# Block-sparse attention and gated MLP on one core: pair 2 before pair 3, block rows by GpSimd as 32-bit words, mask products in one bank, first transposes regrouped

## The chip, the cores and the metric

One core of a Trainium2 chip runs the whole program in one launch. The metric is the device time in microseconds (us). Five engines work side by side, each through its own instructions in order: TensorE (PE, with its weight loads as PEld), VectorE (DVE), ScalarE (ACT), GpSimd (POOL), and SyncE (SP), whose queue here issues nearly all DMA transfers.

## The reference: what is computed

Attention over 4 batches of 8 heads, 768 positions, head size 64, under a block mask (blocks of 32: the neighbours, the first and the last block row and column, and three sampled blocks for each block row), then an MLP with a spatial gate on the 512 joined channels:

```
scores = scale * np.matmul(q, k.transpose(0, 1, 3, 2))
scores = np.where(mask, scores, -1000000000.0)
attn = softmax(scores)                      # over the last axis
x = attn @ v                                # heads joined: (4, 768, 512)
h = np.maximum(x @ w_in, 0.0)               # (4, 768, 1024)
u, v = h[..., :512], h[..., 512:]
v_n = (v - mu) / np.sqrt(var + 1e-06)
v_s = np.einsum('ts,bsd->btd', w_spatial, v_n) + b_spatial[None, :, None]
out = (u * v_s) @ w_out
```

## The kernel before

**Mask in the product.** A tile `kq` holds, for each of 8 head places, k and q transposed: 64 partitions of data (`kq[0:D]`) and 24 more (`MR`, one for each block) with block rows. For k these rows (`K_`) are a one-hot code of the block of each key; for q they are the penalties of that query's block row. A score matmul over 88 partitions then adds the mask by itself. The rows are the same for all heads: they are made for head 0 (`one_hot`, and `mask_rows`, line 295, a matmul with `bm` whose result is copied to `kq[MR, 0, ...]`) and copied to the other heads by `rows` (line 244), on VectorE unless an engine is named. The loads of later pairs reuse the places, so this is done once.

**Units and slots.** Heads go in pairs; pairs 0 to 3 are batch 0. Queries are cut in three thirds (`qcols(0)` to `qcols(2)`, 256 columns each). Batch 0 is worked off in 12 units of 3 slots (`UNITS`, line 426): head 0 and head 1 (thirds 0 and 1), then pairs 1, 2, 3 with third 0, pairs 1 to 3 with third 1, all pairs with third 2. In a slot `qk_unit` (line 429) gives score matmuls into one of two `sc` banks of PSUM and one exponential of 128x1024 on ScalarE (line 450). Slots 0 to 35 are these; the slots behind (`qk_full`, line 452) are the other batches. Slot 6 is the first of pair 1, slot 9 of pair 2, slot 12 of pair 3.

**The order is written by hand.** The main loop (line 845) emits for each slot s: the scores of slot s, the attention products with v that `AV_AT` sets for it (line 839, 8 matmuls for each of three steps of a unit, the third followed by the normalization on VectorE), the functions registered by `when(s, ...)`, the share of the MLP's matmuls that `STEPS` gives, and what is listed as `late`. There is no scheduler: each engine runs what the program gives it in that order, and waits by semaphores.

**From DRAM to `kq`.** `load` (line 105) brings k, q, v of a pair as f32 into staging tiles (`st_k` has 3 buffers, so a fourth k waits until the first has been cast); `cast` (line 119, recorded as L138) makes bf16, mostly on GpSimd. For pairs 1 to 3 `tr_first` (line 383) transposes k and the first third of q on TensorE into one bank (8 transposes, recorded as L290) and VectorE copies it to the two heads' places (two 64x1024 copies, L219); `tr_rest` (line 395) does the other q columns. Pair 0 goes head by head with `head` (L303) and `split0`, in the pieces `second` and `third`. Later pairs are transposed by DMA. `w_in_load` and `w_in_cast` (L235) bring the MLP's first weights through the same queue and through GpSimd; the staging of weights has 6 buffers.

**Start.** Lines 251 to 274 load and cast the first pairs and set the ones column of v (`vv`, memsets); lines 311 to 330 make the first transposes, the mask products (`m0`, `m1` copied by ScalarE, `m2` by VectorE), and the rows of head 1; lines 331 to 361 issue the rest of batch 0's loads and GpSimd's casts in a fixed order, ahead of slot 0 in the program. `filler` gives matmuls on zeros.

Of the kernel before, what the change touches and what calls it, by code (L numbers as in the profile page):

```python
# [26 lines left out]
def kernel(  # L27
# [16 lines left out]
    nc = tc.nc  # L44
# [44 lines left out]
    def qcols(t0, n=1):  # L89
        return slice(S + t0 * TW, S + (t0 + n) * TW)  # L90
# [28 lines left out]
    def cast(p, nm, eng, hs=BOTH, cs=ALLC):  # L119
        if nm == "v":  # L120
            dst = vv[p % NVV][:, hs, cs, 0:D]
        else:
            if p not in nat:
                nat[p] = work.tile([128, 2 * NCH, 2, D], BF16, tag="nat", bufs=4, name="nat")
            c0 = 0 if nm == "k" else NCH
            dst = nat[p][:, c0 + cs.start:c0 + cs.stop].rearrange("p c h d -> p h c d")[:, hs]
        src = st[nm, p].rearrange("p h (c d) -> p h c d", d=D)[:, hs, cs]
        if p == 0 and nm != "v":
            dst = nat0_view()[:, hs, (c0 + cs.start) * D:(c0 + cs.stop) * D]
            if cs is not C45:  # L130
                dst = dst[:, 0].rearrange("p (i t d) -> p t i d", t=2, d=D)
                src = src[:, 0].rearrange("p (t i) d -> p t i d", t=2)
            else:
                dst = dst.rearrange("p h (c d) -> p h c d", d=D)
        if eng is nc.scalar:
            nc.scalar.activation(out=dst, in_=src, func=AF.Copy)
        else:
            eng.tensor_copy(out=dst, in_=src)  # L138
# [92 lines left out]
    def w_in_load(u, g):  # L231
        w_load((u, g), moe_w_in[g * 128:(g + 1) * 128, 0 if u else DH:DH if u else DFF])

    def w_in_cast(u, g, eng):
        eng.tensor_copy(out=w_in_t[:, g, 0 if u else DH:DH if u else DFF], in_=wst.pop((u, g)))  # L235
# [7 lines left out]

    def rows(hs, cs, eng=nc.vector):
        src = kq[MR, 0:1, cs].to_broadcast([NB, hs.stop - hs.start, cs.stop - cs.start])
        if eng is nc.scalar:
            nc.scalar.activation(out=kq[MR, hs, cs], in_=src, func=AF.Copy)
        else:
            eng.tensor_copy(out=kq[MR, hs, cs], in_=src)  # L249

# [3 lines left out]
    load(1, "k")  # L254
    load(1, "q", cs=C01)
    load(0, "v")
    load(3, "k")
    cast(0, "k", PL, H0, C45)
    cast(0, "k", PL, H1)
    cast(0, "q", PL, H1, C03)  # L260
    rows(slice(3, 4), K_, PL)
    load(2, "k")
    load(2, "q", cs=C01)
    load(3, "q", cs=C01)
    load(1, "v")
    load(2, "v")
    load(1, "q", cs=C25)
    for s in range(NVV):
        nc.gpsimd.memset(vv[s][:, :, :, D:VA], 1.0)
    nc.gpsimd.memset(mhalf, -0.5)  # L270
    cast(1, "k", PL)
    cast(1, "q", PL, cs=C01)
    load(3, "v")
    w_in_load(0, 0)

# [10 lines left out]
    def bank(nm="ps", tag=None):  # L286
        return psum.tile([128, 1024], BF16, tag=tag or moe_tag(), bufs=2 if tag else 1, name=nm)
# [5 lines left out]
        return src[:, c].rearrange("p h d -> p (h d)")  # L293

    def mask_rows(ps, t0, n, copy):
        nc.tensor.matmul(out=ps[:, 0:n * TW], lhsT=bm[MR],
                         rhs=kq[MR, 0, t0 * TW:(t0 + n) * TW], start=True, stop=True)
        return lambda: copy(kq[MR, 0, qcols(t0, n)], ps[0:NB, 0:n * TW])


    def head(ps, h, c0, n, at=0):
        for i in range(0, n, 2):
            nc.tensor.transpose(out=ps[:, at + i * 64:at + (i + 2) * 64],  # L303
                                in_=nat0_view()[:, h, (c0 + i) * D:(c0 + i + 2) * D],
                                identity=ident)
# [11 lines left out]
    psq = bank("psq", "av")  # L317
    head(psq, 0, *Q4)
    mq = psum.tile([128, 1024], FP32, tag="sc", bufs=2, name="mq")
    m1 = mask_rows(mq, 1, 1, act_copy)  # L320
    m2 = mask_rows(mq[:, 512:1024], 2, 1, dve_copy)
    split0(ps0, 0, *K4, 0)
    m0()
    split0(ps0, 0, *K4, 1)
    split0(psq, 0, *Q4, 0)
    filler(FILL2, wps)
    split0(psq, 0, *Q4, 1)
    m1()
    m2()
    rows(H1, qcols(0, 3))  # L330
    w_in_load(0, 1)
    load(2, "q", cs=C25)
    w_in_load(0, 2)
    load(0, "q", cs=C45)
    w_in_load(0, 3)
    load(3, "q", cs=C25)
    w_in_load(1, 0)
    w_in_load(1, 1)
    cast(3, "k", PL)
    cast(2, "k", PL)  # L340
    cast(2, "q", PL, cs=C01)
    cast(3, "q", PL, cs=C01)
    cast(1, "v", PL)
    rows(slice(6, 8), qcols(0), PL)
    cast(2, "v", PL)
    cast(1, "q", PL, cs=C25)
    rows(slice(2, 4), qcols(1), PL)
    w_in_cast(0, 0, PL)
    w_in_load(1, 3)
    cast(3, "v", PL)  # L350
    w_in_cast(0, 1, PL)
    w_in_load(1, 2)
    cast(2, "q", PL, cs=C25)
    w_in_cast(0, 2, PL)
    w_in_cast(0, 3, PL)
    cast(3, "q", PL, cs=C25)
    w_in_cast(1, 0, PL)
    w_in_cast(1, 1, PL)
    w_in_cast(1, 2, PL)
    cast(0, "q", PL, cs=C45)  # L360
    w_in_cast(1, 3, PL)

    nc.sync.dma_start(out=b_col, in_=moe_b_spatial.rearrange("(p c) -> p c", c=NCH))
    def second():
        ps2 = bank("ps2", "av")
        head(ps2, 0, *K2)
        for t in range(2):
            split0(ps2, 0, *K2, t)

    def third():  # L370
        ps1 = bank("ps1")
        head(ps1, 1, 0, NCH)
        head(ps1, 1, *Q4, NCH * 64)
# [462 lines left out]
    when(52, *[c(w_out_cast, g, PL) for g in range(NDH)])  # L836

    LAG = 7
    AV_AT = {0: (5, 5, 6), 1: (6, 8, 8), 2: (9, 9, 11), 3: (13, 14, 14), 4: (15, 16, 16), 7: (25, 26, 26), 8: (28, 28, 29), 10: (34, 34, 35)}
    av_at = {}  # L840
    for u in range(len(UNITS)):
        for e in range(3):
# [52 lines left out]
```

## Time and profile before

| | us |
|---|---|
| median of 3 runs | 210.71 |
| the runs | 210.68 to 211.25 |
| profiled execution, its span from first to last instruction | 208.8 |
| around the span (median less span; the profiled execution's own time is listed no further) | 1.9 |
| TensorE busy | 200.8 |
| ScalarE busy | 167.4 |
| VectorE busy | 135.5 |
| GpSimd busy | 71.1 |

How to read the profile: a row of a timeline has the start and the busy time in us, the engine, the line of the kernel, the operation, the tile written and the tile read, their shapes, the count of instructions joined in the row, and in brackets the idle time of that engine ahead of it and what ended it. A row of grouped instructions has the count, then busy time, mean ns of one, and the idle time ahead. TensorE's busy time is modelled and overlaps in its pipeline. The chain that ended last is followed back from the last instruction to what released each step.

### The profile page before, as it was taken

How to read it: one execution, taken by the hardware profiler on the slowest of the kernel's cores; microseconds unless marked ns; L12 is line 12 of the kernel's file. 1: busy time of each engine (PE TensorE's matmuls, PEld its weight loads, DVE VectorE, ACT ScalarE, POOL GpSimd, SP SyncE). 2: the span in 40 equal slices, each digit the busy share in tenths (PEclk: the TensorE clock that was granted, in tenths of full speed). 3: DMA queues.
4: the chain of work that ended last, by engine and by line, in shares of the span. 5: the costliest groups of instructions: out<-in, count | busy, mean ns of one | idle time of the engine just before them, and what ended most of it. 6: DMA issues, size and time to landing. Idle time of an engine off the chain costs nothing.

```text
span 208.8 us, 5242 instructions
## 1 busy us (share of the span) xinstructions
PE 200.8 (96%) x2106; PEld 127.4 (61%) x2140; DVE 135.5 (65%) x295; ACT 167.4 (80%) x221; POOL 71.1 (34%) x110
## 2 busy tenths in 40 slices
PE   8898999999999999999999999999999999999993
PEld 6588878766666666655565555666556556544441
DVE  7999787789664546484986455376785433567542
ACT  4989999999989989989998888979999787266021
POOL 6589699683960422132065031131020000003000
PEclk9999999999999999999999999999999999999999
DMA  5999999999997989799835598894101324520266
GB/s 151 347 365 366 342 395 242 239 308 324 285 302 159 284 242 261 216 321 253 148 142 113 113 224 206 249 284 103 38 3 20 68 53 84 203 106 0 49 149 254
DMA packets 64139, 41.82 MB, mean 200 GB/s; under 512 B 45172, under 2 KB 58868, under 8 KB 64116
## 3 DMA queue, kind: packets, MB, share of 16 engines
q1 hardware_dynamic: 63540, 40.91, 74.9%
q10 hardware_dynamic: 576, 0.59, 0.9%
q8 instruction: 16, 0.26, 0.6%
q14 instruction: 7, 0.06, 0.1%
HBM read 24.38 MB, written 6.29 MB: 147 GB/s over the span
## 4 chain that ended last, share of the span: by engine, by line
PE 88%; DVE 7%; ACT 2%; issue 2%; ACTq 0%
PE ps_moe L583 31%; PE ps L458 22%; PE ps_av L509 12%; PE ps_t L583 8%; PE ps L445 5%; PE ps_sc L583 4%; DVE kq L219 3%; PE ps_av L491 3%; DVE kq L249 2%; PE wps L181 1%; ACT a_all L450 1%; PE ps L290 1%; PE ps_av L290 1%; ACT osb L222 0%; ACT a_all L462 0%
## 5 line engine op out<-in xcount | busy, mean ns | idle before, releaser
L462 ACT ACTIVATE a_all<-ps 128x768 bf16<-128x768 f32 x144 | 113.4, 811 | 14.5 <-PE ps L458 8.2
L458 PE MATMUL ps<-kq 88*128 88x384 bf16 x288 | 70.4, 325 | 0.4
L509 PEld LDWEIGHTS <-a_all 128*128 128x128 bf16 x864 | 45.2, 97 | 20.0
L509 PE MATMUL ps_av<-vv,a_all 128*128 128x65 bf16 x864 | 49.8, 193 | 0.0
L458 PEld LDWEIGHTS <-kq 88*128 88x128 bf16 x288 | 27.7, 98 | 29.7 <-issue 0.2
L583 PE MATMUL ps_moe<-w_in_t,xt 128*128 128x512 bf16 x127 | 38.6, 378 | 0.5
L450 ACT ACTIVATE a_all<-ps 128x1024 bf16<-128x1024 f32 x36 | 34.4, 1024 | 2.3 <-PE ps L445 2.0
L583 PE MATMUL ps_moe<-vn,w_spt 128*128 128x512 bf16 x99 | 30.2, 378 | 0.4
L138 POOL CAST nat<-st_k 128x768 bf16<-128x768 f32 (+2 forms) x17 | 13.6, 803 | 40.5 <-DMA st_k<-in_k_dram 40.2
L622 POOL TENSOR_SCALAR std<-mv 128x3 f32<-128x3 f32 (+1 forms) x9 | 2.1, 238 | 66.1 <-DVE mv L619 46.2
L445 PE MATMUL ps<-kq 88*128 88x256 bf16 (+1 forms) x140 | 21.6, 275 | 1.7 <-DVE kq L219 1.6
L473 DVE RECIPROCAL rc<-ps_av 128x6 f32<-128x6 f32 (+1 forms) x36 | 6.7, 185 | 24.3 <-PE ps_av L509 22.3
L655 DVE SCALAR_TENSOR_TENSOR un<-ps_moe,b_col,un 128x512 bf16<-128x512 f32 x18 | 13.4, 747 | 13.5 <-PE ps_moe L583 11.4
L583 PEld LDWEIGHTS <-xt 128*128 128x128 bf16 x192 | 15.5, 98 | 7.6 <-DVE xt L219 0.2
L583 PE MATMUL ps_moe<-w_out_t,gt 128*128 128x512 bf16 x66 | 19.6, 378 | 0.2
L474 DVE TENSOR_TENSOR xn<-ps_av,rc 128x384 bf16<-128x384 f32 (+1 forms) x36 | 18.5, 513 | 1.2
L618 DVE BATCH_NORM_STATS2 stats<-vn 128x6 f32<-128x512 bf16 x24 | 16.4, 684 | 1.3 <-ACT vn L613 0.9
L219 DVE COPY kq<-tt 64x1536 bf16<-64x1536 bf16 x24 | 16.7, 696 | 0.3
L138 POOL CAST nat<-st_q 128x768 bf16<-128x768 f32 (+2 forms) x21 | 15.0, 716 | 4.5 <-DMA st_q<-in_q_dram 4.5
L445 PEld LDWEIGHTS <-kq 88*128 88x128 bf16 x140 | 12.5, 97 | 5.5 <-DVE kq L219 1.8
L583 PEld LDWEIGHTS <-w_spt 128*128 128x128 bf16 x144 | 11.6, 98 | 5.6
L138 POOL CAST vv<-st_v 128x768 bf16<-128x768 f32 x15 | 13.1, 875 | 3.7 <-DMA st_v<-in_v_dram 2.4
(82 smaller groups left out, 207.4 us busy)
## 6 DMA issues: line engine op xcount, KB each, us to landing
st_v<-in_v_dram SPq DMA_DIRECT2D x16, 384.0 KB, 6.0
st_k<-in_k_dram SPq DMA_DIRECT2D x15, 384.0 KB, 4.9
out_dram<-osb SPq DMA_DIRECT2D x22, 256.0 KB, 3.4
st_q<-in_q_dram SPq DMA_DIRECT2D x12, 384.0 KB, 4.8
ws_f<-in_moe_w_spatial_dram SPq DMA_DIRECT2D x6, 384.0 KB, 7.3
w_f<-in_moe_w_in_dram SPq DMA_DIRECT2D x8, 256.0 KB, 5.7
w_f<-in_moe_w_out_dram SPq DMA_DIRECT2D x4, 256.0 KB, 4.2
st_q<-in_q_dram SPq DMA_DIRECT2D x6, 128.0 KB, 5.5
```

The lines of the kernel that those rows point to most:

```text
L138: eng.tensor_copy(out=dst, in_=src)
L219: nc.vector.tensor_copy(out=o, in_=i)
L445: nc.tensor.matmul(out=ps[:, at:at + n * TW], lhsT=kq[:, h, ci * 128:(ci + 1) * 128], rhs=kq[:, h, qcols(t0, n)], start=True, stop=True)
L450: nc.scalar.activation(out=out, in_=ps, func=AF.Exp, scale=0.125)
L458: nc.tensor.matmul(out=ps[:, hf * 512:hf * 512 + HALF], lhsT=kq[:, j % H, ci * 128:(ci + 1) * 128], rhs=kq[:, j % H, S + hf * HALF:S + (hf ...
L462: nc.scalar.activation(out=a_ref["h", j][:, ci, :].rearrange("p (b c) -> p b c", b=2), in_=ps.rearrange("p (b c) -> p b c", b=2)[:, :, 0:H ...
L473: nc.vector.reciprocal(out=rc[:, 0:n], in_=ps[:, :, D:VA])
L474: nc.vector.tensor_tensor(out=out, in0=ps[:, :, 0:D], in1=rc[:, 0:n].to_broadcast([128, n, D]), op=ALU.mult)
L509: nc.tensor.matmul(out=av_ref[j][:, qc, 0:VA], lhsT=a_ref["h", j][:, ci, qc * 128:(qc + 1) * 128], rhs=vv[p % NVV][:, h, ci, 0:VA], start= ...
L583: nc.tensor.matmul(out=ref["ps"][:, 0:w], lhsT=lhs(i), rhs=rhs(i), start=(i == 0), stop=(i == n - 1))
L618: nc.vector.bn_stats(out=stats, in_=self.vn[:, tcc, :])
L655: nc.vector.scalar_tensor_tensor(out=self.un[:, tcc, :], in0=ps, scalar=b_col[:, tcc:tcc + 1], in1=self.un[:, tcc, :], op0=ALU.add, op1=AL ...
```

## The change

- Pair 2's k is loaded before pair 3's, and its k and q are cast before pair 3's on GpSimd.
- `rows` on GpSimd copies 32-bit words (two bf16 columns as one I32). The rows of heads 1 to 5 (k rows of heads 2 to 5, q rows of heads 1 to 5 in the first third, head 1 in all thirds) go from VectorE to GpSimd; head 1's k rows stay on VectorE, and head 3's k rows were on GpSimd already. The k rows of heads 6 and 7 stay on VectorE and move from slot 7 to slot 1.
- The mask products of thirds 1 and 2 go to one bank, and one ScalarE copy takes both; VectorE's copy `m2` is gone. `mask_rows` gives one matmul for each third.
- Pair 0's second q cast on GpSimd comes behind head 1's q rows; the `vv` memsets and pair 1's casts come further back in the program text, in the order below.
- The long block of loads and casts becomes `staged`, called at slot 1; the load of the bias (`b_col`) stands ahead of it.
- `third` is cut in two, k at slot 0 and q at slot 1. Pair 1's first transposes are one group at slot 4 (were two, slots 3 and 4), pair 3's are at slot 9 (was 10). The attention products of units 1 and 2 move from slots 6, 8, 8 and 9, 9, 11 to 8, 8, 10 and 11, 11, 12.

```diff
     def rows(hs, cs, eng=nc.vector):
         src = kq[MR, 0:1, cs].to_broadcast([NB, hs.stop - hs.start, cs.stop - cs.start])
-        if eng is nc.scalar:
-            nc.scalar.activation(out=kq[MR, hs, cs], in_=src, func=AF.Copy)
+        if eng is PL:
+            w = (cs.stop - cs.start) // 2
+            eng.tensor_copy(out=kq[MR, hs, cs].bitcast(I32),
+                            in_=kq[MR, 0:1, cs].bitcast(I32).to_broadcast(
+                                [NB, hs.stop - hs.start, w]))
...
-    load(3, "k")
+    load(2, "k")
     cast(0, "k", PL, H0, C45)
     cast(0, "k", PL, H1)
-    cast(0, "q", PL, H1, C03)
     rows(slice(3, 4), K_, PL)
-    load(2, "k")
     load(2, "q", cs=C01)
+    load(3, "k")
     load(3, "q", cs=C01)
...
-    for s in range(NVV):
-        nc.gpsimd.memset(vv[s][:, :, :, D:VA], 1.0)
-    nc.gpsimd.memset(mhalf, -0.5)
-    cast(1, "k", PL)
-    cast(1, "q", PL, cs=C01)
...
     def mask_rows(ps, t0, n, copy):
-        nc.tensor.matmul(out=ps[:, 0:n * TW], lhsT=bm[MR],
-                         rhs=kq[MR, 0, t0 * TW:(t0 + n) * TW], start=True, stop=True)
+        for i in range(n):
+            nc.tensor.matmul(out=ps[:, i * TW:(i + 1) * TW], lhsT=bm[MR],
+                             rhs=kq[MR, 0, (t0 + i) * TW:(t0 + i + 1) * TW],
+                             start=True, stop=True)
...
-    m1 = mask_rows(mq, 1, 1, act_copy)
-    m2 = mask_rows(mq[:, 512:1024], 2, 1, dve_copy)
+    m12 = mask_rows(mq, 1, 2, act_copy)
...
-    m1()
-    m2()
-    rows(H1, qcols(0, 3))
+    m12()
+    rows(H1, qcols(0, 3), PL)
+    cast(0, "q", PL, H1, C03)
+    rows(slice(2, 3), K_, PL)
+    for s in range(NVV):
+        nc.gpsimd.memset(vv[s][:, :, :, D:VA], 1.0)
+    nc.gpsimd.memset(mhalf, -0.5)
+    rows(slice(2, 4), qcols(0), PL)
+    cast(1, "k", PL)
+    cast(1, "q", PL, cs=C01)
+    rows(slice(4, 6), K_, PL)
+    rows(slice(4, 6), qcols(0), PL)
+    nc.sync.dma_start(out=b_col, in_=moe_b_spatial.rearrange("(p c) -> p c", c=NCH))
+    def staged():
...
-    cast(3, "k", PL)
-    cast(2, "k", PL)
-    cast(2, "q", PL, cs=C01)
-    cast(3, "q", PL, cs=C01)
+        cast(2, "k", PL)
+        cast(2, "q", PL, cs=C01)
+        cast(3, "k", PL)
+        cast(3, "q", PL, cs=C01)
...
-    def third():
-        ps1 = bank("ps1")
-        head(ps1, 1, 0, NCH)
+    def third_k():
+        head1["ps"] = bank("ps1")
+        head(head1["ps"], 1, 0, NCH)
+        for t in range(2):
+            split0(head1["ps"][:, 0:NCH * 64], 1, 0, NCH, t)
+
+    def third_q():
+        ps1 = head1.pop("ps")
         head(ps1, 1, *Q4, NCH * 64)
-        for c0, n, at in ((0, NCH, 0), (*Q4, NCH * 64)):
-            for t in range(2):
-                split0(ps1[:, at:at + n * 64], 1, c0, n, t)
+        for t in range(2):
+            split0(ps1[:, NCH * 64:(NCH + 2 * TC) * 64], 1, *Q4, t)
...
-    ROWS = [(1, 2, 4, qcols(0)), (1, 2, 3, K_), (4, 4, 6, qcols(0)), (6, 4, 6, K_), (7, 6, 8, K_), (15, 4, 8, qcols(1)), (22, 2, 8, qcols(2))]
+    ROWS = [(1, 6, 8, K_), (15, 4, 8, qcols(1)), (22, 2, 8, qcols(2))]
     when(0, second)
-    when(1, third)
+    when(0, third_k)
+    when(1, third_q)
...
-    when(3, c(tr_first, 1, 0, 4))
-    when(4, c(tr_first, 1, 4))
+    when(4, c(tr_first, 1))
...
-    when(10, c(tr_first, 3))
+    when(9, c(tr_first, 3))
...
+    when(1, staged)
...
-    AV_AT = {0: (5, 5, 6), 1: (6, 8, 8), 2: (9, 9, 11), 3: (13, 14, 14), ...}
+    AV_AT = {0: (5, 5, 6), 1: (8, 8, 10), 2: (11, 11, 12), 3: (13, 14, 14), ...}
```

More of the change, by code (lines that the diff above doesn't have):

```diff
@@ L327 @@
     split0(psq, 0, *Q4, 1)
-    m1()
-    m2()
-    rows(H1, qcols(0, 3))
[L331 to L338, printed above, removed]
-    cast(3, "k", PL)
-    cast(2, "k", PL)
-    cast(2, "q", PL, cs=C01)
-    cast(3, "q", PL, cs=C01)
[L343 to L361, printed above, removed]
-    nc.sync.dma_start(out=b_col, in_=moe_b_spatial.rearrange("(p c) -> p c", c=NCH))
+    m12()
[10 more added lines that the diff above has]
+    rows(slice(4, 6), qcols(0), PL)
+    nc.sync.dma_start(out=b_col, in_=moe_b_spatial.rearrange("(p c) -> p c", c=NCH))
+    def staged():
+        w_in_load(0, 1)
+        load(2, "q", cs=C25)
+        w_in_load(0, 2)
+        load(0, "q", cs=C45)
+        w_in_load(0, 3)
+        load(3, "q", cs=C25)
+        w_in_load(1, 0)
+        w_in_load(1, 1)
+        cast(2, "k", PL)
+        cast(2, "q", PL, cs=C01)
+        cast(3, "k", PL)
+        cast(3, "q", PL, cs=C01)
+        cast(1, "v", PL)
+        rows(slice(6, 8), qcols(0), PL)
+        cast(2, "v", PL)
+        cast(1, "q", PL, cs=C25)
+        rows(slice(2, 4), qcols(1), PL)
+        w_in_cast(0, 0, PL)
+        w_in_load(1, 3)
+        cast(3, "v", PL)
+        w_in_cast(0, 1, PL)
+        w_in_load(1, 2)
+        cast(2, "q", PL, cs=C25)
+        w_in_cast(0, 2, PL)
+        w_in_cast(0, 3, PL)
+        cast(3, "q", PL, cs=C25)
+        w_in_cast(1, 0, PL)
+        w_in_cast(1, 1, PL)
+        w_in_cast(1, 2, PL)
+        cast(0, "q", PL, cs=C45)
+        w_in_cast(1, 3, PL)
     def second():
@@ L368, in second @@
             split0(ps2, 0, *K2, t)
-    def third():
-        ps1 = bank("ps1")
-        head(ps1, 1, 0, NCH)
+    head1 = {}
+    def third_k():
[5 more added lines that the diff above has]
+        ps1 = head1.pop("ps")
         head(ps1, 1, *Q4, NCH * 64)
-        for c0, n, at in ((0, NCH, 0), (*Q4, NCH * 64)):
-            for t in range(2):
-                split0(ps1[:, at:at + n * 64], 1, c0, n, t)
+        for t in range(2):
+            split0(ps1[:, NCH * 64:(NCH + 2 * TC) * 64], 1, *Q4, t)
     def mask_last():
@@ L838 @@
     LAG = 7
-    AV_AT = {0: (5, 5, 6), 1: (6, 8, 8), 2: (9, 9, 11), 3: (13, 14, 14), 4: (15, 16, 16), 7: (25, 26, 26), 8: (28, 28, 29), 10: (34, 34, 35)}
+    AV_AT = {0: (5, 5, 6), 1: (8, 8, 10), 2: (11, 11, 12), 3: (13, 14, 14), 4: (15, 16, 16), 7: (25, 26, 26), 8: (28, 28, 29), 10: (34, 34, 35)}
     av_at = {}
```

## The prediction

> **What bounds the kernel now.** I read the page first, for the span and the chain that ended last, then ScalarE's timeline from 0 to 60 us for the places where the chain changes hands.
>
> ```profile
> span 208.8 us, 5242 instructions
> ...
> PE 88%; DVE 7%; ACT 2%; issue 2%; ACTq 0%
> ```
>
> TensorE is the chain for 88% of the span; VectorE holds 7%, some 15 us. The change touches only the first third, so the question is where those 15 us lie. ScalarE's timeline, whose exponentials (L450) set one slot each, shows it:
>
> ```profile
> 5.14 0.37 ACT L222 ACTIVATE kq<-mq 24x256 bf16<-24x256 f32 x1 [0.38 <-PE mq L296]
> 5.81 8.66 ACT L450 ACTIVATE a_all<-ps 128x1024 bf16<-128x1024 f32 x9 [0.30 <-PE ps L445]
> 15.04 2.85 ACT L450 ACTIVATE a_all<-ps 128x1024 bf16<-128x1024 f32 x3 [0.57 <-PE ps L445]
> 18.25 9.69 ACT L450 ACTIVATE a_all<-ps 128x1024 bf16<-128x1024 f32 x10 [0.35 <-PE ps L445]
> 28.23 4.89 ACT L450 ACTIVATE a_all<-ps 128x1024 bf16<-128x1024 f32 x5 [0.29 <-PE ps L445]
> ```
>
> Slots 0 to 8 run without a gap: 8.66 / 9 = 0.962 us each. Then 0.57 us is lost ahead of slot 9 (first of pair 2) and 0.35 ahead of slot 12 (first of pair 3). Each waits for scores, and TensorE's timeline says what those wait for; VectorE's timeline says why that is late:
>
> ```profile
> 14.33 0.61 PE L445 MATMUL ps<-kq 88*128 88x256 bf16 x4 [0.46 <-DVE kq L219]
> ...
> 17.54 0.61 PE L445 MATMUL ps<-kq 88*128 88x256 bf16 x4 [0.54 <-DVE kq L219]
> ```
>
> ```profile
> 3.54 0.34 DVE L249 COPY kq<-kq 24x768 bf16<-24x768 bf16 x1
> ...
> 8.38 1.07 DVE L249 COPY kq<-kq 24x512 bf16<-24x512 bf16 x2
> 9.48 0.56 DVE L138 CAST vv<-st_v 128x768 bf16<-128x768 f32 x1
> 10.08 1.41 DVE L219 COPY kq<-ps 64x1024 bf16<-64x1024 bf16 x2
> 11.52 0.81 DVE L249 COPY kq<-kq 24x512 bf16<-24x512 bf16 x1
> ...
> 13.01 0.55 DVE L249 COPY kq<-kq 24x1536 bf16<-24x1536 bf16 x1
> 13.59 1.41 DVE L219 COPY kq<-ps 64x1024 bf16<-64x1024 bf16 x2
> 15.03 1.19 DVE L249 COPY kq<-kq 24x1536 bf16<-24x1536 bf16 x1
> ```
>
> From 8.4 on VectorE has no idle time in these rows (the brackets that would name one are missing), and block-row copies (L249) stand directly ahead of the pair copies that the scores of slots 9 and 12 need. Behind 18.25 ScalarE runs ten slots in a row, and from there the chain is TensorE:
>
> ```profile
> 24.07 2.04 ACT a_all L450 x2
> ...
> 26.15 0.60 PE ps L445 x4
> ```
>
> ```profile
> 18.25:28.23 9.98, 9.78 (x155) 8.39 (x155) 8.21 (x23) 9.57 (x11) 7.86 (x14) 1.00 1.03 362
> ```
>
> The first fence is of the chain in order of time: two exponentials, then TensorE, which the chain hardly leaves again. In the second, one stretch of ten us (busy us of PE, PEld, DVE, ACT, POOL, then clock and DMA share) TensorE is idle 0.2 of 9.98 us. So what the first 18 us give is not absorbed later: the end moves by what slot 12 moves, if no supply is missed.
>
> **The change part by part.**
>
> (a) *Row copies off VectorE.* Between 8.4 and 16.2 us VectorE sheds 1.07 (two copies), 0.81 and 0.55; the 1.19 one (heads 6 and 7) moves to slot 1, where VectorE waits for TensorE. That is 1.07 + 0.81 + 0.55 + 1.19 = 3.6 us, against a lag of 0.57 + 0.35. VectorE stops being what ends last.
>
> (b) *The same copies on GpSimd.* The trace has no 32-bit word copy. Rows that bound it:
>
> ```profile
> L138 POOL CAST nat<-st_k 128x384 bf16<-128x384 f32 x1 | 0.5, 507 | 0.1
> ```
>
> ```profile
> 4.09 0.93 POOL L138 CAST nat<-st_k 128x128 bf16<-128x128 f32 x2
> 6.15 0.46 POOL L138 CAST nat<-st_q 128x256 bf16<-128x256 f32 x1 [1.13 <-DMA st_q<-in_q_dram]
> 6.67 0.82 POOL L249 COPY kq<-kq 24x768 bf16<-24x768 bf16 x1
> 7.55 0.40 POOL L269 MEMSET vv<- 128x12 bf16 x6
> ...
> 8.02 0.82 POOL L138 CAST nat<-st_k 128x768 bf16<-128x768 f32 x1
> 8.78 0.46 POOL L138 CAST nat<-st_q 128x256 bf16<-128x256 f32 x1
> 10.26 0.83 POOL L138 CAST nat<-st_k 128x768 bf16<-128x768 f32 x1 [1.02 <-DMA st_k<-in_k_dram]
> 11.35 0.83 POOL L138 CAST nat<-st_k 128x768 bf16<-128x768 f32 x1 [0.27 <-DMA st_k<-in_k_dram]
> 12.12 0.80 POOL L138 CAST nat<-st_q 128x256 bf16<-128x256 f32 x2
> ```
>
> 768 elements cost 0.82 whether they are 2-byte copies or 4-byte reads, and 384 cost 0.51: the price goes by elements, (0.82 - 0.51) / 384 = 0.8 ns each. The nearest row, the 384-element cast, reads words of the same width; I take 0.50 for 384 words, 0.42 for 256, 0.82 for 768. Low end: the 0.34 of VectorE's 24x768 copy at 3.54, which moves the same bytes. High end: words cost by bytes, 0.82 for 384.
>
> GpSimd's new order by these prices, all estimates: rows of head 3 from the end of the pair-0 casts, 5.02 to 5.5; rows of head 1, which now wait for the joint mask copy (c) at 5.75, 5.8 to 6.3; pair 0's second q cast 6.3 to 6.75 (was 6.15 to 6.61; its data came at 6.13, so this wait mostly replaces another); rows of head 2, 0.5, to 7.2; the memsets, 0.47 from 7.55 to 8.02, to 7.7; q rows of heads 2 and 3, 0.42, to 8.1. So pair 1's casts start at 8.05 where they started at 8.02: the shed bf16 copy (0.82) and the 1.13 and 1.02 us of idle pay for them. Then rows of heads 4 and 5, 0.82 + 0.42, from 9.25 to 10.4, in what was a DMA wait. Two later copies, now words too, drop from 0.61 to 0.42. The block put into a function and called at slot 1 keeps its order on every queue; only the bias load goes ahead of it.
>
> Queued behind GpSimd's new wait for ScalarE is the second q cast, and for it wait two transposes, then slot 2's scores. The row before:
>
> ```profile
> 6.89 0.59 PE L445 MATMUL ps<-kq 88*128 88x512 bf16 x2
> ```
>
> By the estimate they start at 6.95 and end at 7.55; slot 2's exponential is due at 5.81 + 2 x 0.962 = 7.73. Hidden with 0.2 us to spare; past that each 0.1 costs 0.1.
>
> (c) *Mask products in one bank.* Same three products. ScalarE now copies 24x512 at once instead of 24x256 (0.37), VectorE loses one. For a 512-wide PSUM read on ScalarE the trace has
>
> ```profile
> 46.47 0.59 ACT L649 ACTIVATE un<-ps_moe 128x512 bf16<-128x512 f32 x1
> ```
>
> so 5.14 + 0.59 = 5.73, inside ScalarE's idle 0.30 before 5.81. Slot 0 is not moved. Bounds: 0 to 0.1 late.
>
> (d) *Pair 2 ahead of pair 3.* The same bytes in another order. Pair 3's k, issued first, landed just before its cast at 10.26, pair 2's before 11.35; they change places. On SP's queue the load that waits for a staging buffer, formerly pair 2's k, is now pair 3's, behind pair 2's q; nothing more waits behind it. So pair 2's casts run 10.4 to 11.2 and 11.2 to 11.6 (ended 12.5), pair 3's 11.6 to 12.4 and to 12.8 (k ended 11.1, q 12.9). Slot 7's transposes of pair 2 go at 12.05, VectorE copies head 4 by 13.3, and slot 9's scores are then held by the score bank, free when slot 7's exponential ends at 13.5. Slot 9 is due at 5.81 + 9 x 0.962 = 14.47, scores ready 14.15. **The 0.57 goes.** Pair 3's transposes, at slot 9 instead of 10, run near 14.0, its two copies by 15.9; slot 12's scores are needed by 17.35 and start at 16.4. **The 0.35 goes.**
>
> (e) *Regrouped transposes and later attention products.* The work of TensorE is unchanged; units 1 and 2 move their products two slots later. Pieces of the chain give the prices (four scores, eight products, four transposes):
>
> ```profile
> 20.41 0.45 PE ps L445 x4
> 20.85 0.24 PE ps_av L491 x8
> 21.10 0.23 PE ps L290 x4
> ```
>
> Slot 12 then holds scores 0.44, products 0.24, and 8 transposes 0.45, together 1.13 against a slot of 0.962; slot 11 holds 0.93 and slot 13 0.79, and a slot's scores have 0.3 us of lead, so this costs nothing while the lead stands, 0.17 without it.
>
> (f) *What is late next.* With slot 12 at 17.33 instead of 18.25, all work paced by slots comes 0.92 earlier; what DMA paces does not. One supply is that tight:
>
> ```profile
> 24.94 0.61 POOL L235 CAST w_in_t<-w_f 128x512 bf16<-128x512 f32 x1 [1.95 <-DMA w_f<-in_moe_w_in_dram]
> 25.50 0.40 POOL L138 CAST nat<-st_q 128x256 bf16<-128x256 f32 x1
> ```
>
> ```profile
> 26.83 0.27 PE L303 MATMUL ps_av<-ident,nat 128*128 128x128 bf16 x2
> ```
>
> Slot 21's two transposes at 26.83 need the cast that ends at 25.90, itself behind a weight cast that GpSimd awaited 1.95 us from DMA. Moved 0.92 they would start at 25.91. With 0.05 of hand-over they start near 25.95; the bias load, now issued ahead of those weights, has 3 KB against their 256 KB, for which I allow up to 0.1 more. I take 0.1 us lost in all.
>
> Sum: -0.57 - 0.35 + 0.1 = -0.82, a span of 208.0. The median of the three runs, 210.71, stands 1.9 above the profiled span (the profiled execution's own time is listed no further); with the same 1.9, 209.9.
>
> [...] The row first: the two 24x1536 copies on VectorE took 0.55 at 13.01 and 1.19 at 15.03, the latter while GpSimd was casting:
>
> ```profile
> 15.76 0.94 POOL L138 CAST nat<-st_q 128x512 bf16<-128x512 f32 x1
> ```
>
> This 512-element cast took 0.94 beside that copy; the one at 24.94 above, as wide, took 0.61. [...]
>
> **The rivals.**
>
> *Collision.* Two SBUF copies stay on VectorE beside GpSimd's denser stretch: rows of heads 6 and 7 near 7.7, and v's cast near 9.2. By the pair 0.55/1.19 and 0.61/0.94, VectorE may lose 0.64 and GpSimd 0.33 each. Then pair 1's q cast ends 9.6 to 9.9 instead of 9.24, slot 5's scores (due 10.62, ready about 10.2) slip by up to 0.1, and slot 6's by up to 0.3. Time: 209.9 + 0.1 to 0.4, say 210.2. For it: the rows above. Against: the pair copies read PSUM and kept 1.41 for two beside GpSimd's casts.
>
> *A late supply.* If the weight load of (f) lands 0.5 later through the reordering, slot 21 gives back most of the gain: 210.4. Against: the bytes ahead of it are the same.
>
> *Slower: GpSimd becomes the bound.* Up to pair 2's casts it copies 384 x 3 + 256 x 2 + 768 = 2432 words. At 1.7 ns a word (by bytes, the high end) pair 0's q cast slips to 7.1, pair 1's to 10.2 and pair 2's to 13.7; gaps of 0.24, 0.14 and 0.63 before slots 2, 5 and 8 replace 0.92: 210.8 and no change. From there each further 0.4 ns a word costs 2432 x 0.4 = 1.0 us: at 2.1 ns, 211.8. For it: no 32-bit copy in the trace. Against: a 4-byte read costs GpSimd no more than a 2-byte one.
>
> *More.* ScalarE's gap of 0.29 at 28.23 also closes, if TensorE comes in with a longer lead: 209.5. Against: slot 21's work and bank limits are unchanged.
>
> **How the numbers follow.** Forecast 0.55, collision and late supply together 0.26, GpSimd as the bound 0.14 (0.04 of it near 210.8), more 0.05. About 0.3% (0.63 us) is what a measurement of this kernel can tell from no change: faster means below 210.08, slower above 211.34. Forecast and more give faster 0.60; collision, late supply and the mild end of the bound give same 0.30; the rest of the bound slower 0.10. The range runs from 209.4 (the "more" case) to 211.0 (the bound by bytes and 0.2), leaving out 0.1 for a bound beyond bytes and some 0.05 below. The likeliest case alone is 209.6 to 210.1.
>
> **What would show it.** Right: no idle piece on ScalarE between slots 0 and 21, slot 12's exponential near 17.3, GpSimd's 24x384 word copies near 0.50, pair 2's k cast ahead of 10.6, VectorE with idle time between 9 and 17. (f) shows as a TensorE wait for GpSimd near 25.9. Wrong: word copies at 0.8 or more, a gap before slots 2, 5 or 6, pair 1's casts later than 8.3, or a slot 12 that moves while the span does not.

## The result and the profile after

The changed kernel takes 218.12 us (median of 6 runs, 217.24 to 219.31), the kernel before 210.69 (6 runs, 210.21 to 211.38): a ratio of 1.034, 95% interval 1.031 to 1.037. The forecast was 209.9, so it missed by 8 us and on the wrong side. The page of the changed kernel, its span and the chain that ended last:

```profile
span 216.3 us, 5278 instructions
...
PE 88%; POOL 5%; DVE 2%; DMA 2%; issue 1%; SPq 1%; ACT 0%; POOLq 0%; ACTq 0%
```

VectorE's share of the chain fell from 7% to 2%, as the change would have it. GpSimd (POOL), which the chain before did not list, now holds 5%. ScalarE's timeline of the changed kernel (its exponentials of slots 0 to 35 are at L465) shows the places:

```profile
5.36 0.58 ACT L222 ACTIVATE kq<-mq 24x512 bf16<-24x512 f32 x1 [0.60 <-PE mq L294]
6.43 1.02 ACT L465 ACTIVATE a_all<-ps 128x1024 bf16<-128x1024 f32 x1 [0.49 <-PE ps L460]
...
12.88 1.95 ACT L465 ACTIVATE a_all<-ps 128x1024 bf16<-128x1024 f32 x2 [0.62 <-PE ps L460]
17.62 1.02 ACT L465 ACTIVATE a_all<-ps 128x1024 bf16<-128x1024 f32 x1 [2.78 <-PE ps L460]
19.32 1.02 ACT L465 ACTIVATE a_all<-ps 128x1024 bf16<-128x1024 f32 x1 [0.68 <-PE ps L460]
21.12 1.02 ACT L465 ACTIVATE a_all<-ps 128x1024 bf16<-128x1024 f32 x1 [0.78 <-PE ps L460]
22.77 11.57 ACT L465 ACTIVATE a_all<-ps 128x1024 bf16<-128x1024 f32 x12 [0.62 <-PE ps L460]
34.63 4.88 ACT L465 ACTIVATE a_all<-ps 128x1024 bf16<-128x1024 f32 x5 [0.29 <-PE ps L460]
...
48.66 1.02 ACT L465 ACTIVATE a_all<-ps 128x1024 bf16<-128x1024 f32 x1 [1.01 <-PE ps L460]
```

Before, slots 0 to 8 ran without a gap from 5.81. Here slots 5 and 6 are the pair at 12.88, slot 7 starts at 17.62 and slot 10 at 22.77. From there twelve run in a row: the gap before slot 12 is gone, but 6.8 us too late. TensorE's timeline says why:

```profile
7.95 1.06 PE L460 MATMUL ps<-kq 88*128 88x512 bf16 x2
...
13.96 0.38 PE L460 MATMUL ps<-kq 88*128 88x256 bf16 x2
16.97 0.61 PE L460 MATMUL ps<-kq 88*128 88x256 bf16 x2 [2.63 <-POOL kq L248]
...
18.23 1.06 PE L460 MATMUL ps<-kq 88*128 88x256 bf16 x4
```

Slot 7 has four score matmuls, two for head 2 and two for head 3. The first two run at 13.96; the other two wait 2.63 us for a row copy by GpSimd. The same trace by its waits has this wait once, with no other of its kind:

```profile
PE ps L460 <- POOL kq L248: 2.6, 1, 2.6
```

GpSimd's timeline shows which copy ends it:

```profile
7.03 0.50 POOL L248 COPY kq<-kq 24x384 int32<-24x384 int32 x1
...
8.51 0.82 POOL L138 CAST nat<-st_k 128x768 bf16<-128x768 f32 x1
...
10.07 1.37 POOL L248 COPY kq<-kq 24x768 int32<-24x768 int32 x2
11.51 0.82 POOL L138 CAST nat<-st_k 128x768 bf16<-128x768 f32 x1
...
16.52 0.39 POOL L248 COPY kq<-kq 24x256 int32<-24x256 int32 x1
```

The copy at 16.52 ends at 16.91, and the scores go at 16.97. It is the last row copy in `staged`: `rows(slice(2, 4), qcols(1), PL)`, the q rows of heads 2 and 3 in the **second** third. Slot 7 belongs to pair 1 with the **first** third, and reads nothing that this copy writes. The wait is needless. In the program of the changed kernel the third weight load of slot 7 waits for VectorE and GpSimd; in the kernel before it waited for VectorE alone, although GpSimd made the same copy there, as bf16. So the wait is written into the program, and the chip only keeps it.

The wait costs more than itself. By stretches of one microsecond (busy us of PE, PEld, DVE, ACT, POOL, then the granted clock, DMA share, GB/s):

```profile
15.00:16.00 1.00, 0.00 (x0) 0.00 (x0) 0.00 (x0) 0.00 (x0) 0.94 (x3) 1.00 1.12 368
16.00:17.00 1.00, 0.03 (x1) 0.03 (x2) 0.00 (x0) 0.00 (x0) 0.87 (x3) 0.57 1.01 350
...
22.00:23.00 1.00, 1.00 (x13) 0.81 (x12) 0.97 (x2) 0.38 (x2) 0.94 (x2) 0.52 1.10 374
23.00:24.00 1.00, 1.00 (x25) 0.95 (x23) 0.92 (x3) 1.00 (x2) 0.29 (x1) 1.00 1.03 373
```

While TensorE idles the granted clock falls to 0.50 (from about 16.1, by the 0.57 over the stretch from 16), and it is back only at about 22.9 (by the 0.52 over the stretch from 22), although TensorE is full again from 17. Four scores take 1.06 us at 18.23 instead of 0.60. The clock fell some 1.8 us after TensorE's last matmul ahead of the wait (13.96 + 0.38 = 14.34), while the wait was still on.

Two smaller losses stand beside this. Up to 13 us TensorE's matmuls took their doubled time (1.06 for two 88x512 scores at 7.95; 0.59 in the kernel before), though the granted clock reads 1.00 there. And near 47 us one slot is late by 1.0; there two SBUF operations of VectorE took long beside casts on GpSimd (the same copy took 0.56 at 47.74, without one); that the casts made them long was not tested:

```profile
43.36 3.45 POOL L570 CAST ws_b<-ws_f 128x768 bf16<-128x768 f32 x2
43.48 1.92 DVE L219 COPY kq<-tt 64x1536 bf16<-64x1536 bf16 x1
...
45.33 1.64 DVE L187 TENSOR_SCALAR vn<-vn,mv,rstd 128x512 bf16<-128x512 bf16 x1
...
47.21 0.65 PE L506 MATMUL ps_av<-vv,a_all 128*128 128x65 bf16 x16 [0.95 <-DVE xt L219]
```

The account of this one execution, as lag of the changed kernel behind the one before at the same slot: slot 6 is at 12.88 + 0.97 = 13.85 against 5.81 + 6 x 0.962 = 11.58, so +2.27 (the slow start). Slot 7 is +5.08: the wait adds 2.81. Slots 7 to 10 take 5.15 against three slots of 0.962, 2.26 lost at half clock; since the kernel before lost 0.57 in the same slots, the lag grows by 1.70, to 6.78. Without the 0.35 before slot 12 it is 6.4 at slot 22 (34.63 against 28.23), and with the 1.0 near 47 us it is 7.4, of 7.5 between the spans.

### The profile page after: what moved, and what is told of

Read it like the earlier page. It is cut to its first block, busy times and chain, and to the rows that moved or that the text cites. A ratio compares the mean times of both kernels' runs of the same rounds, so it can differ in the third digit from the quotient of the medians.

```text
span 216.3 us, 5278 instructions
## 1 busy us (share of the span) xinstructions
PE 208.3 (96%) x2140; PEld 131.3 (61%) x2140; DVE 133.8 (62%) x289; ACT 168.1 (78%) x221; POOL 72.7 (34%) x115
## 4 chain that ended last, share of the span: by engine, by line
PE 88%; POOL 5%; DVE 2%; DMA 2%; issue 1%; SPq 1%; ACT 0%; POOLq 0%; ACTq 0%
PE ps_moe L598 32%; PE ps L473 22%; PE ps_av L524 12%; PE ps_t L598 7%; PE ps L460 6%; PE ps_av L506 4%; PE ps_sc L598 3%; POOL nat L138 2%; DMA st_q<-in_q_dram 2%; POOL kq L248 2%; PE ps L287 2%; DVE vn L187 1%; DVE kq L219 1%; POOL vv L138 1%; PE ps_av L287 0%
## 5 line engine op out<-in xcount | busy, mean ns | idle before, releaser
L524 PEld LDWEIGHTS <-a_all 128*128 128x128 bf16 x864 | 45.2, 97 | 20.0
L473 PEld LDWEIGHTS <-kq 88*128 88x128 bf16 x288 | 27.7, 98 | 29.7 <-issue 0.2
L598 PE MATMUL ps_moe<-w_in_t,xt 128*128 128x512 bf16 x144 | 43.2, 378 | 0.0
L465 ACT ACTIVATE a_all<-ps 128x1024 bf16<-128x1024 f32 x36 | 34.9, 1025 | 8.9 <-PE ps L460 8.6
L598 PE MATMUL ps_moe<-vn,w_spt 128*128 128x512 bf16 x108 | 32.7, 378 | 0.0
L460 PE MATMUL ps<-kq 88*128 88x256 bf16 (+1 forms) x140 | 25.9, 313 | 2.6 <-POOL kq L248 2.6
L598 PE MATMUL ps_moe<-w_out_t,gt 128*128 128x512 bf16 x72 | 21.0, 378 | 0.0
L460 PEld LDWEIGHTS <-kq 88*128 88x128 bf16 x140 | 14.1, 108 | 7.1 <-POOL kq L248 2.9
L219 DVE COPY kq<-tt 64x1536 bf16<-64x1536 bf16 x24 | 17.8, 743 | 0.3
L219 DVE COPY kq<-ps 64x1024 bf16<-64x1024 bf16 (+4 forms) x20 | 8.9, 447 | 10.1 <-PE ps L287 8.1
L506 PEld LDWEIGHTS <-a_all 128*128 128x128 bf16 x288 | 13.3, 101 | 2.9 <-issue 1.7
```

What stands on the lines that cost most here:

```text
L219: nc.vector.tensor_copy(out=o, in_=i)
L460: nc.tensor.matmul(out=ps[:, at:at + n * TW], lhsT=kq[:, h, ci * 128:(ci + 1) * 128], rhs=kq[:, h, qcols(t0, n)], start=True, stop=True)
L465: nc.scalar.activation(out=out, in_=ps, func=AF.Exp, scale=0.125)
L473: nc.tensor.matmul(out=ps[:, hf * 512:hf * 512 + HALF], lhsT=kq[:, j % H, ci * 128:(ci + 1) * 128], rhs=kq[:, j % H, S + hf * HALF:S + (hf ...
L506: nc.tensor.matmul(out=av_ref[u][:, to, 0:VA], lhsT=a_ref[u][:, at:at + 128], rhs=vv[pp % NVV][:, h, ci, 0:VA], start=(ci == 0), stop=(ci ...
L524: nc.tensor.matmul(out=av_ref[j][:, qc, 0:VA], lhsT=a_ref["h", j][:, ci, qc * 128:(qc + 1) * 128], rhs=vv[p % NVV][:, h, ci, 0:VA], start= ...
```

## The experiments

**The theory:** the row copy on words over two heads, placed ahead of slot 7's scores in the program, is taken for something that these scores read, though it writes other columns; the wait and the clock that it pulls down are the loss. **Rivals:** GpSimd is too slow for what it was given, or the regrouped TensorE work made the loss.

**The copy emitted later.** From the changed kernel: the second half of `staged`, from that copy on, is emitted at slot 8, behind slot 7's scores. The order on every engine stays.

```
+    def staged_tail():
         rows(slice(2, 4), qcols(1), PL)
...
+    when(8, staged_tail)
```

> The changed kernel with the second half of staged (from the q rows of heads 2 and 3 in the second third on) written into the program behind slot 8 instead of slot 1. Every engine runs the same instructions in the same order as in the changed kernel; only what waits for what can differ. Theory (needless wait): the changed kernel's slot 7 holds its third score weight load until GpSimd's 24x256 word copy that starts at 16.52, though head 3's scores of the first third read nothing that this copy writes; with the copy written later the 2.6 us wait is gone, TensorE has no idle stretch near 14.3 to 17, so its granted clock stays 1.00, and the time falls by 4 us or more, to between 209.9 (if the start is also as in the kernel before) and 213 (if the first 13 us stay as slow as in the changed kernel). Rival (GpSimd is really late): TensorE waits for GpSimd at another place, near 17, and the time stays above 216.

Measured: 211.24 against 210.68, ratio 1.002 (0.998 to 1.006). The same GpSimd copies in the same order, and 6.9 us are gone. ScalarE's timeline of this run:

```profile
8.17 1.02 ACT L467 ACTIVATE a_all<-ps 128x1024 bf16<-128x1024 f32 x1 [0.68 <-PE ps L462]
9.45 18.12 ACT L467 ACTIVATE a_all<-ps 128x1024 bf16<-128x1024 f32 x19 [0.26 <-PE ps L462]
```

Slots 3 to 21 run without a gap, so both old gaps, before 9 and 12, are closed. But 0.68 and 0.26 are lost before slots 2 and 3.

**The copy cut by heads.** From the changed kernel, that one copy as two copies of one head each, still on words, still in its place:

```
-        rows(slice(2, 4), qcols(1), PL)
+        rows(slice(2, 3), qcols(1), PL)
+        rows(slice(3, 4), qcols(1), PL)
```

> The changed kernel with that one word copy (q rows of heads 2 and 3, second third) made as two copies, one for each head. Theory: what makes the wait is the two-head word copy, whose span from head 2 to head 3 takes in head 3's k and first third; head by head it takes in nothing else, so the wait goes as in e1 and the time is that of e1 within 0.5 us, with one GpSimd instruction more (two of about 0.3 us for one of 0.39). Rival (any GpSimd word copy written ahead of slot 7 holds it): the wait stays, 217 to 219.

Measured: 210.45 against 210.68, ratio 1.001 (0.997 to 1.005). One line more, one GpSimd instruction more, and the whole loss is gone in the median; the regrouped TensorE work is still all there, so that rival falls. ScalarE, then TensorE with GpSimd and VectorE ahead of it, then TensorE's stretches in this run:

```profile
5.98 1.94 ACT L466 ACTIVATE a_all<-ps 128x1024 bf16<-128x1024 f32 x2
8.46 1.02 ACT L466 ACTIVATE a_all<-ps 128x1024 bf16<-128x1024 f32 x1 [0.55 <-PE ps L461]
9.74 18.14 ACT L466 ACTIVATE a_all<-ps 128x1024 bf16<-128x1024 f32 x19 [0.26 <-PE ps L461]
28.18 4.89 ACT L466 ACTIVATE a_all<-ps 128x1024 bf16<-128x1024 f32 x5 [0.29 <-PE ps L461]
```

```profile
6.52 0.40 POOL L138 CAST nat<-st_q 128x256 bf16<-128x256 f32 x1
```

```profile
6.04 1.19 DVE L219 COPY kq<-ps 64x128 bf16<-64x128 bf16 x4 [0.44 <-PE ps L302]
```

```profile
7.28 0.29 PE L302 MATMUL ps<-ident,nat 128*128 128x128 bf16 x2 [0.68 <-DVE kq L219]
```

```profile
6.00:8.00 2.00, 1.32 (x11) 0.77 (x9) 1.51 (x6) 1.92 (x2) 1.76 (x10) 0.85 0.94 329
8.00:10.00 2.00, 2.00 (x12) 1.34 (x11) 1.85 (x3) 1.28 (x2) 1.92 (x3) 0.50 1.08 360
```

What is left to explain: slot 22 at 28.18 is where it was before (28.23). Both old gaps are closed (0.92), and the start gives it back: TensorE waits 0.68 before the two transposes that stand ahead of slot 2's scores, the clock falls to 0.50 at about 7.4, and slot 3 is at 9.74 where before it was at 5.81 + 3 x 0.962 = 8.70. The wait has two parts. Pair 0's second q cast ends at 6.92; then VectorE, until 7.23, still copies head 1's k out of the bank that these transposes write, because `third` was cut in two. In the program of the kernel before, the same transposes wait for no copy of VectorE. The half clock is that of the profiled execution: its mean clock is 0.992, and the other nine of the ten runs have 1.000.

**Words alone, in the kernel before.** From the kernel before, only the form of its three GpSimd row copies:

```
-        if eng is nc.scalar:
-            nc.scalar.activation(out=kq[MR, hs, cs], in_=src, func=AF.Copy)
+        if eng is PL:
+            w = (cs.stop - cs.start) // 2
+            eng.tensor_copy(out=kq[MR, hs, cs].bitcast(I32), ...)
```

> The kernel before, with one edit: its three block-row copies on GpSimd are 32-bit words. Theory (needless wait): the two-head word copy of the second third (at 16.76 in the kernel before) now holds slot 7's third weight load, which ran near 12.3; a wait of about 4 us for GpSimd before slot 7, the granted clock falls to 0.50 for some us, and the time is 214 to 218. Rival (the new order of GpSimd's work is what is late, words are harmless): the same as the kernel before within 0.5 us, each word copy 0.2 to 0.3 us shorter.

Measured: 221.38, ratio 1.052 (1.045 to 1.059), worse than expected. VectorE's and ScalarE's timelines of this run:

```profile
17.15 0.55 DVE L252 COPY kq<-kq 24x512 bf16<-24x512 bf16 x2 [8.80 <-POOL kq L248]
```

```profile
20.57 1.02 ACT L453 ACTIVATE a_all<-ps 128x1024 bf16<-128x1024 f32 x1 [8.48 <-PE ps L448]
```

The word form alone, with nothing else of the change, makes the wait; here it falls on VectorE, whose first row copies behind slot 1 (heads 2 and 3, first third) wait 8.80 us for GpSimd's copy of the same heads in the second third, which ends at 17.11 in this trace. They write other columns. The rival of a slow GpSimd falls: its word copies are shorter than the bf16 ones (0.39 and 0.61 for the same rows). Two heads as bf16, in the kernel before, and one head as words, in the run ahead of this one, make no such wait: it takes both, words and two heads in one copy. Why is then argued, not shown: the copy is tracked by its whole span of addresses, and from head 2's q to head 3's q in the second third that span holds head 3's k and first third, which slot 7's scores read and VectorE's copy writes. It fits that in the changed kernel the two scores of head 2, whose columns lie outside the span, ran at 13.96, and only those of head 3 waited.

**The idle time bridged.** From the changed kernel, 40 matmuls on zeros ahead of slot 7's scores: `when(6, ... filler(40, ...))`.

> The changed kernel with 40 matmuls on zeros (128x128) ahead of slot 7's scores, so that TensorE is busy for some 2.2 us of its 2.6 us wait. Theory (the wait costs twice: once itself, once by the clock): slot 8 starts no earlier than before the edit, but the granted clock stays 1.00 from 16 to 23 us, the matmul groups there take 0.60 us where they took 1.06, and about 2.4 us come back: 215.7. Rival (the clock costs nothing, the exponentials set the pace): 218 as in the changed kernel, or 2 us more if the added matmuls push slot 7 back.

Measured: 215.41 (four runs, 215.06 to 217.71), ratio 1.027 (1.018 to 1.036). TensorE, its stretches, and ScalarE in this run:

```profile
17.37 0.39 PE L460 MATMUL ps<-kq 88*128 88x256 bf16 x2 [0.97 <-POOL kq L248]
```

```profile
16.00:18.00 2.00, 1.03 (x16) 0.73 (x13) 0.00 (x0) 0.21 (x1) 1.87 (x5) 1.00 1.05 356
```

```profile
17.79 14.34 ACT L465 ACTIVATE a_all<-ps 128x1024 bf16<-128x1024 f32 x15 [3.04 <-PE ps L460]
```

The wait stands and slot 7 is as late, yet from slot 7 on the exponentials run without a gap: the clock stays 1.00, and 2.7 us come back in the median. So the needless wait costs once for itself and once through the clock. Two of the four runs have a mean clock of 1.000 (215.06 and 215.26), the others 0.989 (215.55) and 0.992 (217.71); these two were not profiled. And TensorE stood idle 0.97 us here without a fall of the clock.

**The start kept busy.** From the version with the heads apart, 8 matmuls on zeros in slot 1 (`when(1, keep_busy)`), to keep the clock up in slots 1 to 3.

> The kernel with heads apart (the changed kernel without its needless wait), plus 8 matmuls on zeros ahead of head 1's q transposes in slot 1, where TensorE stood idle 0.7 us. There the clock then fell to 0.50 at about 7.4 us for 3.4 us. Theory (that idle stretch is what lowers the clock): with it filled the clock stays 1.00 through 12 us, slots 2 and 3 lose 0.2 to 0.4 us instead of 0.8, and the median falls 0.4 to 1.0 below that of heads apart (210.45). [...]

Measured: 211.87 against 210.73, ratio 1.005 (1.002 to 1.008): slower, against the expectation. ScalarE at the start, then TensorE and SP's queue at the end, in this run, and last SP's queue in the kernel before:

```profile
5.75 21.26 ACT L466 ACTIVATE a_all<-ps 128x1024 bf16<-128x1024 f32 x22
27.31 4.89 ACT L466 ACTIVATE a_all<-ps 128x1024 bf16<-128x1024 f32 x5 [0.29 <-PE ps L461]
```

```profile
204.74 0.61 PE L599 MATMUL ps_sc<-w_out_t,gt 128*128 128x256 bf16 x4 [1.21 <-DMA gt<-un]
```

```profile
201.70 4.47 SPq L700 DMA_DIRECT2D out_dram<-osb  x5
```

```profile
202.62 3.33 SPq L684 DMA_DIRECT2D out_dram<-osb  x5
```

The start does what the prediction said of the whole change: 22 slots without a gap and slot 22 at 27.31, 0.92 earlier. The tail gives it back: TensorE waits 1.21 us for the transposes of `gt`, and SP takes 4.47 us to issue five stores, 3.33 in the kernel before. The profiled execution is the fastest of the twelve (210.67); the median stands 1.2 above it.

**The cast first.** From the version with the heads apart, pair 0's second q cast ahead of head 1's rows, the other way to help slot 2:

> The kernel with heads apart, with pair 0's second q cast put back ahead of head 1's row copy on GpSimd, as the kernel before has it. Theory (the joint mask copy and the row copy behind it hold that cast): the cast starts near 6.1 instead of 6.5, TensorE waits 0.35 us less in slot 1, slot 2's exponential starts 0.3 to 0.6 earlier, median 0.3 to 0.6 below heads apart. Rival (the data's landing holds the cast): no change.

Measured: 210.42, ratio 1.001 (0.998 to 1.004). No TensorE wait is listed at the start any more, but the profiled execution ran its matmuls at the doubled time up to 12.7 us, so what it brings can't be read from it. **Both together:**

> Heads apart with both edits of the start: the q cast first and the 8 matmuls. Theory: the clock stays 1.00, slot 2 loses nothing, and the forecast of 209.9 is met, 0.5 to 1.0 below the kernel before. Rival (the start costs for another reason, the joint mask copy): 210.4 to 211.

Measured: 211.90, ratio 1.007 (1.005 to 1.010), with the loss in the tail again (a wait of 1.65 for `gt`). The cast ends at 6.45 here, and still the transposes wait for VectorE's copies:

```profile
7.21 0.27 PE L302 MATMUL ps<-ident,nat 128*128 128x128 bf16 x2 [0.22 <-DVE kq L219]
```

So the order on GpSimd alone does not free them.

**A part of the change, in the kernel before.** Pair 2 ahead of pair 3, and the rows of heads 4 and 5 (first third, and k) as words on GpSimd behind pair 1's casts; nothing else:

```
-        if eng is nc.scalar:
+        if eng is PL and hs.start == 4:
...
-    load(3, "k")
+    load(2, "k")
...
+    rows(slice(4, 6), K_, PL)
+    rows(slice(4, 6), qcols(0), PL)
     cast(2, "k", PL)
     cast(2, "q", PL, cs=C01)
+    cast(3, "k", PL)
```

> The kernel before, with one part of the change alone: pair 2 loaded and cast ahead of pair 3, and the rows of heads 4 and 5 (k rows and first third) by GpSimd as words, in the stretch where it waited for data, in place of VectorE's two copies in slots 4 and 6. Start, mask products, transposes and attention products as before; the word copies' spans take in nothing that is used before slot 9. Theory (the forecast's gain was real and the start ate it): the gaps ahead of slots 9 and 12 go (0.57 and 0.35), the start is that of the kernel before, 209.8 to 210.1 where the kernel before has 210.7. Rival (VectorE is not what makes the gaps): within 0.3 us of the kernel before.

Measured: 210.12 against 210.73, ratio 0.999 (0.997 to 1.002): not told from no change. Its profiled execution has a span of 207.7:

```profile
5.77 21.09 ACT L455 ACTIVATE a_all<-ps 128x1024 bf16<-128x1024 f32 x22 [0.30 <-PE ps L450]
27.15 4.88 ACT L455 ACTIVATE a_all<-ps 128x1024 bf16<-128x1024 f32 x5 [0.29 <-PE ps L450]
```

Both gaps are closed, and in this pair of executions the 1.1 us are kept to the end (207.7 against 208.8). These copies take in two heads as words too, but stand where nothing that follows waits needlessly. Of all versions this has the lowest median; the times of 12 runs, 209.40 to 212.34, spread too far to prove the 1 us.

**What made the tail late.** The runs with a late tail had 16 rows more in TensorE's stream, and one more transfer of instructions on queue 8. Three runs: the kept-busy version with eight zero matmuls taken away elsewhere (four at the start, the four of slot 2), so that the count is that of the heads apart; the heads apart with eight more in slot 2; and the kernel before with eight more in slot 2.

> The run with eight zero matmuls in slot 1, with eight taken away elsewhere (four of the 24 at the start, the four of slot 2), so that TensorE has as many instructions as in the version with the heads apart, and the work of the reference is unchanged. Theory, instruction count: the loss of 1.2 us in the tail (TensorE waits 1.21 for the transposes of gt, five stores take 4.47 us to issue) came with a 17th transfer of instructions on queue 8, which 16 more rows of TensorE's stream needed; here the queue has 16 transfers, the five stores take 3.33, no wait of TensorE is listed behind 202 us, and with exponentials without a gap up to slot 21 the span is 207.6 to 208.0, the time 209.5 to 210.0. Rival, earlier slots meet a fixed tail: the wait stays at about 1.2 and the time near 211.9. Third case: with four fewer zero matmuls at the start the rate of TensorE comes up at another moment, exponentials start up to 1 us later; then the tail alone is to be read.

> The version with the heads apart, with 12 zero matmuls in slot 2 where there were 4: 16 more rows of TensorE's stream, none in slot 1. Theory, instruction count: 17 transfers on queue 8, the tail's five stores take 4.4 us or more to issue, TensorE waits 1.2 or more for gt, the time is 211.4 to 212.3. Rival, the place of the matmuls or earlier slots: 16 transfers and the tail as with the heads apart (3.33), time 210.2 to 211.0.

> The kernel before with 12 zero matmuls in slot 2 where it has 4, and nothing else. Theory, instruction count: 17 transfers on queue 8 and a tail longer by 1.1 to 1.7 us although no slot comes earlier: 211.6 to 212.6. Rival, earlier slots meet a fixed tail: the slots are where they were, so at most the half microsecond of the eight matmuls is lost: 210.6 to 211.2 with 16 transfers, five stores in 3.33 us.

Measured: 212.27, 213.07 and 212.11 against 210.92; ratios 1.006 (1.002 to 1.010), 1.008 (1.004 to 1.011) and 1.006 (1.003 to 1.008). All three profiled executions began with matmuls at the doubled time, up to 10 us (the kernel before with more in slot 2) and up to 12 us and more (the other two), so the tail alone is read: the page's row of queue 8 (transfers, MB, share) and SP's stores. Same count:

```profile
q8 instruction: 16, 0.26, 0.6%
...
205.64 3.35 SPq L700 DMA_DIRECT2D out_dram<-osb  x5
```

The heads apart, and more in slot 2:

```profile
204.38 4.85 SPq L700 DMA_DIRECT2D out_dram<-osb  x5
```

The kernel before, and more in slot 2 (queue 8, SP, TensorE):

```profile
q8 instruction: 17, 0.28, 0.6%
...
204.50 4.75 SPq L684 DMA_DIRECT2D out_dram<-osb  x5
...
207.82 0.61 PE L583 MATMUL ps_sc<-w_out_t,gt 128*128 128x256 bf16 x4 [1.45 <-DMA gt<-un]
```

In these profiles the tail goes with the count. With 16 transfers it is whole, though the zero matmuls stand in slot 1; with 17 it is late by 1.2 to 1.65 us, in the kernel before too, where no slot comes earlier. The part made in the kernel before is the counterpart: its slots come 1.08 earlier, it has 16 transfers, and its five stores take 3.33. So the rival, that earlier slots meet a fixed tail, falls. The place counts as well: with 40 more matmuls (the bridged run) there are 17 transfers too, but the last comes between 197 and 199 us, ahead of the stores, and those take 3.33. In the four late tails it comes between 201 and 207, among them. That this transfer is what holds SP's stores is inferred from its place; how one transfer of 0.28 / 17 = 0.016 MB would do so was not tried. The same-count run's time does not bear this out by itself: with four zero matmuls fewer at the start its lowest run is 210.79, 209.55 for the heads apart and 210.80 for the heads apart with 17 transfers.

## Why the prediction was wrong, point by point

- **The step that failed** is in (b): "The block put into a function and called at slot 1 keeps its order on every queue; only the bias load goes ahead of it", and, of the two later copies in it, "now words too, drop from 0.61 to 0.42". The order was kept and the price was right (0.39). What changed is who waits for them: one of them became something that slot 7's scores wait for, by 2.6 us. Cutting it by heads takes 7.7 us off (218.12 to 210.45). Of these the account above puts 2.8 on the wait, 1.7 on the clock and 1.0 on the slot near 47 us; the slow start, 2.3 in the account, is missing in the profile of the heads apart, and whether the copy has a part in it stays open. I priced the words as work on GpSimd and as a new wait of GpSimd; I did not ask whose waits the new form of the copy would change. None of the rivals held this.
- **The clock** was in no term. I took TensorE's durations as fixed; the clock was 0.50 for 6.8 us, and bridging the idle time gave back 2.7.
- **(a) Copies off VectorE:** right. Both gaps, 0.57 and 0.35, are closed in every version without the needless wait, and slot 22 came 0.92 earlier in the kept-busy run and 1.08 earlier in the part made in the kernel before.
- **(b) Prices on GpSimd:** right for 384 words (0.50 forecast and measured) and 256 (0.42 and 0.39). Heads 4 and 5 took 1.37 instead of 1.24, and pair 1's q cast 0.72 instead of 0.46, while VectorE was copying too: it fits the rival of a collision, in a small way, and was not tested. Pair 1's casts began at 8.51 instead of 8.05 and pair 2's k at 11.51 instead of 10.4, in a start that was itself slow. The rival of GpSimd as the bound is refuted.
- **(b) "Hidden with 0.2 us to spare"** before slot 2: wrong in the profiled executions. In the version with the heads apart TensorE waits 0.68 there, and at the half clock that follows slot 3 is 1.04 late, which eats the whole gain of 0.92. The cast ended at 6.92, forecast 6.75; the rest is VectorE's copies up to 7.23, a wait that came with cutting `third` in two and that no term held. The bound "past that each 0.1 costs 0.1" was too kind, for the clock.
- **(c) The joint mask copy:** its price was right (0.58, forecast 0.59). In executions that came to the full rate early slot 0 started between 5.55 (the copy emitted later) and 5.98 (the heads apart), against 5.81: at most 0.17 late, the bound was 0.1.
- **(d), (e), (f):** right as far as they show, but for `third` above. With the needless wait gone (the copy emitted later, the heads apart), slots 3 to 21 run without a gap; no late supply at slot 21 and no loss at slots 11 to 13.
- **The sum:** the gain of 0.82 to 1.1 exists in profiles, but no run proves it against 0.3%. The lowest run of the kernel before, 209.28, is no slower than the lowest of any version (209.40, the part made in the kernel before), and the version with the heads apart ends level with the kernel before.

## What to carry to other kernels

When a copy changes its element type or its grouping, look at the waits of everything that follows on the same tile, not only at its price: here one copy over two heads, as words, held up work that touches none of what it writes, for 2.63 us in the changed kernel and for 8.80 in the kernel before with words, and one copy per head, or a later place in the program, took the 2.63 away. On TensorE ask of an idle stretch whether it costs twice, once for itself and once for a half clock behind it: here 0.68 us did in one execution, and 0.97 us in another did not. And when a version loses at a place that it doesn't touch, compare the transfers of instructions, their number and their place (17 against 16 here, and 1.2 to 1.65 us), before you look for a cause in the change.

## What the runs showed of the hardware that was not expected

- The clock fell after short idle times: some 1.8 us in the changed kernel, and 0.68 us in the version with the heads apart, in a stretch in which TensorE was busy 1.32 of 2 us. The length of the idle time alone did not decide: 0.97 us in the bridged run left the clock at 1.00.
- At the start the granted clock reads 1.00 while matmuls take their doubled time, and the moment at which this ends differs between executions of the same stream. The version with the heads apart and the one with eight more zero matmuls in slot 2 are the same up to slot 2; slot 0's scores took 0.61 us in the one and 1.06 in the other, and in the latter they stayed so to about 12.5 us, although TensorE was busy 3.89 of the 4 us from 4 to 8. Slot 0 then starts 0.45 later (6.43 against 5.98). It fits the runs of one kernel, which for the heads apart fall into six from 209.55 to 210.48 and four from 211.82 to 212.24, but that was not tested: what sets the moment stays open, and with it whether the changed kernel's slow start is its own.
- Sixteen more rows in TensorE's stream went with one more transfer of instructions and, where that fell between 201 and 207 us, with 1.2 to 1.65 us at the other end of the kernel. Eighty more rows, in the bridged run, also brought one more transfer, at 197 to 199 us, and the five stores took 3.33.
